# G formed in two runs of 1280 and 1024 columns from one W tile, where there were three pairs of 384

## The chip, the core and the metric

The kernel runs on one core of a Trainium2 chip. The core has five engines with queues of their own: TensorE (PE, matrix products into PSUM; PEld are its weight loads), VectorE (DVE), ScalarE (ACT), GpSimd (POOL, which also issues transfers) and SyncE (SP, which issues transfers and transposing transfers). They wait for each other through semaphores. The metric is the device time of one execution in microseconds (us), median over several runs; lower is better.

## What is computed

Two stages in one kernel. The first is attention between a sequence `x` (8 batches, 8 heads, 512 rows of 64) and a small state (32 rows per head); the second is a feed-forward layer with a maximum over three products, over 8 x 544 = 4352 rows:

```
scores  = x @ state.T / 8;   a  = softmax(scores);    xread = a  @ state
scores2 = state @ x.T / 8;   a2 = softmax(scores2);   sread = a2 @ x
rows    = concat(xread, sread), the heads side by side: 512 columns
h       = max(rows @ w1, rows @ w2, rows @ w3)        # 768 columns
out     = h @ w_out                                   # 512 columns
```

## The kernel before

The work goes batch by batch. The x rows take a short cut: `rows @ w_i` is `a @ (state @ w_i)`. So for each batch the kernel first forms **G**, the product of the state with w1, w2 and w3, and then multiplies the attention weights `a` with G.

*G.* The 768 columns of h are taken in six groups m of 128, and the three matrices i side by side, so G of a batch is 128 rows (4 heads x 32 state rows) by 2 halves g by 2304 columns. `g_cols(b, ms)` (L240) forms the columns of the groups in `ms`, 384 per group. Per group it takes a PSUM buffer of the tag "two" (two buffers, each of two banks), runs 8 matmuls of 64 rows by 32 columns (4 pairs of heads s, 2 halves g) that sit on different parts of the array (`tile_position`), and has ACT copy 128x768 to G in bf16. `defer` lets such a copy wait: it goes into `copies_due` and is run behind the next t0 copy in `maxout` (L291), or by `flush_copies` at the next `g_cols`. `g_cols_fast` (L263), used twice for batch 0, takes two buffers of the tag "pw" (four buffers of one bank) and has ACT copy one half and DVE the other.

*W.* The weights lie in four tiles `w_sb`, for the groups (0), (1), (2,3) and (4,5); in each, matrix i is a block of 128 or 256 columns. `w_cols(m)` gives the tile and the slice, and `load_w` (L90) loads them by POOL's queue, one transfer per matrix and tile.

*Products.* `x_maxout(b, m)` (L296) makes three products of 512 columns from G and the transposed weights aT into three "pw" buffers (`pw0`, `pw1`, `pw2`), each of two matmuls. ACT copies the first (t0, L290), DVE takes the maximum with the second (t1, L293) and with the third (ht, L294). `s_maxout(m)` does the same for the state rows of all batches at the end. `ffn_out(b, j)` (L306) multiplies ht with w_out in six matmuls into a "pw" buffer; ACT copies it to `osb` (L326), and POOL sends two such pieces off at a time.

*Attention.* `scores` (L165) multiplies x, transposed, with `bd`, the state laid out in blocks, into a "two" buffer, and ACT takes the exponential e. `softmax` sums on DVE (den, rden) and multiplies on POOL (a). `a_transpose_dma` turns a by a transposing transfer on SP. `sread` (L213) makes the state's read into a "pw" buffer, and DVE divides it (L227, L229). For batches 4 to 7 `states` (L129) turns the state by a transposing transfer, and POOL copies it into `bd` (L140).

*Order.* The order of all instructions is written out by hand. Batches 0 and 1 are started together, with transfers still coming in (L344 to L423). Then a loop over b = 2 to 7 (L426) has six slots: `x_maxout(b, m)` and, behind it, the pieces of slot m. With n = b + 1: slot 0 has `scores(n)`; slot 1 `softmax(n)`, `g_cols(b, (2, 3))` and `ffn_out(b-1, 0)`; slot 2 the transposing transfers, `g_cols(b, (4, 5))` and `ffn_out(b-1, 1)`; slot 4 `ffn_out(b-1, 2)`, `sread(n)` and `g_cols(n, (0, 1))`; slot 5 `ffn_out(b-1, 3)`. So G of a batch is formed in three pairs, the first of them ahead of the batch. For batch 2 the first pair stands in the written order (L411). In the last turn there is no next batch, and `s_maxout(m)` fills each slot.

Each engine runs its instructions in this order. A buffer of a tag is given again to a later tile once its last reader is done, so the tags "two" and "pw" make PE wait for copies.

Of the kernel before, what the change touches and what calls it, by code (L numbers as in the profile page):

```python
# [8 lines left out]
F32 = mybir.dt.float32  # L9
BF16 = mybir.dt.bfloat16  # L10
# [5 lines left out]
def kernel(  # L16
# [14 lines left out]
    nc = tc.nc  # L31

    B, H, S, D = x.shape
    _, _, Ns, _ = state.shape
# [8 lines left out]
    HS = H // 2  # L43
    NM = d_ff // 128
# [5 lines left out]
    wpool = ctx.enter_context(tc.tile_pool(name="weights", bufs=1))  # L50
    work = ctx.enter_context(tc.tile_pool(name="work", bufs=2))
    pp = ctx.enter_context(tc.tile_pool(name="pp", bufs=2, space=bass.MemoryType.PSUM))
    ctx.enter_context(tc.manual_schedule())
    dve, act, pool = nc.vector.tensor_copy, nc.scalar.copy, nc.gpsimd.tensor_copy
# [29 lines left out]
    nc.gpsimd.dma_start(out=x0_sb[1], in_=x0_heads(1))  # L84

    chunks = ((0, 1), (1, 2), (2, 4), (4, 6))
    w_sb = [wpool.tile([128, HS, 3, (m1 - m0) * 128], BF16, name=f"w{m0}") for m0, m1 in chunks]
    wout_sb = wpool.tile([128, NM, d_model], BF16, name="wout")

    def load_w(c, parts=(0, 1, 2)):  # L90
        m0, m1 = chunks[c]
        for i in parts:
            w = (moe_w1, moe_w2, moe_w3)[i]
            nc.gpsimd.dma_start(  # L94
                out=w_sb[c][:, :, i, :],
                in_=w.rearrange("(kk p) f -> p kk f", p=128)[:, :, m0 * 128:m1 * 128])

    def w_cols(m):
        c = [m0 <= m < m1 for m0, m1 in chunks].index(True)
        f = (m - chunks[c][0]) * 128  # L100
        return w_sb[c], slice(f, f + 128)

    load_w(0)
    load_w(1)
# [8 lines left out]
    ats = data.tile([128, B, HS, Ns], BF16, name="ats")  # L113
# [7 lines left out]
    def bd(b, h):  # L121
        return bds[b // 2][:, b % 2, h]
# [21 lines left out]
    xT, e, a, aT, G, ht, osb = {}, {}, {}, {}, {}, {}, {}  # L144

    def new(d, b, shape, name, bufs=2):
        d[b] = work.tile(shape, BF16, tag=name, bufs=bufs, name=name)
# [13 lines left out]
    def x_transpose_dma(b):  # L161
        new(xT, b, [128, H, 2, 128], "xT", bufs=3)
        nc.sync.dma_start_transpose(out=xT[b].rearrange("p h j t -> p (h j) t"), in_=x_sb[b][:, 0:XW])
# [42 lines left out]
    def a_transpose_dma(b):  # L206
        new(aT, b, [128, J, 2, 128], "aT", bufs=3)
        nc.sync.dma_start_transpose(
            out=aT[b].rearrange("p j g t -> p (j g) t"), in_=a[b].rearrange("p j g s n -> p (j g s n)"))
# [3 lines left out]
    def sread(b):  # L213

        p = pp.tile([128, 2, 2, D], F32, tag="pw", bufs=4, name="psr")
        for j in range(J):
            for g in range(2):
                for s in range(HS):
                    xj = xv[b][:, 2 * s + g, j, :]
                    both = bass.AP(xj.tensor, xj.offset,  # L220
                                   (xj.ap[0], (XW - ((2 * s + g) * J + j) * D, 2), (1, D)))
                    nc.tensor.matmul(  # L222
                        p[32 * s:32 * s + 32, g], e[b][:, j, g, s, :], both,
                        start=(j == 0 and g == 0), stop=(j == J - 1), skip_group_check=True,
                        tile_position=(0, 32 * s))
        rd = work.tile([128, 2, 1], F32, tag="rd", name="rd")
        nc.vector.reciprocal(out=rd, in_=p[:, :, 1, 0:1])  # L227
        sr = work.tile([128, 2, D], BF16, tag="sr", bufs=B, name="sr")
        nc.vector.tensor_mul(out=sr, in0=p[:, :, 0, :], in1=rd.to_broadcast((128, 2, D)))  # L229
        late.append(lambda: nc.sync.dma_start_transpose(  # L230
            out=ats[:, b].rearrange("p s n -> p (s n)"), in_=sr.rearrange("p g d -> p (g d)")))


    copies_due = []

    def flush_copies():
        while copies_due:
            copies_due.pop(0)()

    def g_cols(b, ms, copies=(nc.scalar.copy, nc.scalar.copy), defer=(False, False)):  # L240

        flush_copies()
        for m, copy, wait in zip(ms, copies, defer):
            if m == 0:
                new(G, b, [128, 2, NM * 384], "G", bufs=3)
            w, f = w_cols(m)
            p = pp.tile([128, 2, 512], F32, tag="two", name="pg")
            for s in range(HS):
                for g in range(2):
                    nc.tensor.matmul(  # L250
                        p[32 * s:32 * s + 32, g, 0:384].rearrange("p (i f) -> p i f", i=3),
                        bd(b, 2 * s + g)[64 * g:64 * g + 64, g, :], w[64 * g:64 * g + 64, s, :, f],
                        start=True, stop=True, tile_position=(64 * g, 32 * s))

            def place(m=m, p=p, copy=copy):
                copy(out=G[b][:, :, m * 384:(m + 1) * 384], in_=p[:, :, 0:384])  # L256

            if wait:
                copies_due.append(place)
            else:  # L260
                place()

    def g_cols_fast(b, m):  # L263

        if m == 0:
            new(G, b, [128, 2, NM * 384], "G", bufs=3)
        w, f = w_cols(m)
        p = [pp.tile([128, 512], F32, tag="pw", bufs=4, name=f"pgf{g}") for g in range(2)]
        for s in range(HS):
            for g in range(2):  # L270
                nc.tensor.matmul(
                    p[g][32 * s:32 * s + 32, 0:384].rearrange("p (i f) -> p i f", i=3),
                    bd(b, 2 * s + g)[64 * g:64 * g + 64, g, :], w[64 * g:64 * g + 64, s, :, f],
                    start=True, stop=True, tile_position=(64 * g, 32 * s))
        for g, copy in ((0, act), (1, dve)):
            copy(out=G[b][:, g, m * 384:(m + 1) * 384], in_=p[g][:, 0:384])  # L276


    def maxout(b, m, n, lhs, rhs, nk):
        if m == 0:  # L280
            new(ht, b, [128, NM, n], "ht", bufs=4)
        pw = []
        for i in range(3):
            p = pp.tile([128, 512], F32, tag="pw", bufs=4, name=f"pw{i}")
            for k in range(nk):
                nc.tensor.matmul(p[:, 0:n], lhs(i, k), rhs(k), start=(k == 0), stop=(k == nk - 1))  # L286
            pw.append(p)
        t0 = work.tile([128, 512], BF16, tag="t0", name="t0")
        t1 = work.tile([128, 512], BF16, tag="t1", name="t1")
        nc.scalar.copy(out=t0[:, 0:n], in_=pw[0][:, 0:n])  # L290
        if copies_due:  # L291
            copies_due.pop(0)()
        nc.vector.tensor_max(t1[:, 0:n], t0[:, 0:n], pw[1][:, 0:n])  # L293
        nc.vector.tensor_max(ht[b][:, m, :], t1[:, 0:n], pw[2][:, 0:n])  # L294

    def x_maxout(b, m):  # L296
        maxout(b, m, 512,
               lambda i, k: G[b][:, k, m * 384 + i * 128:m * 384 + i * 128 + 128],
               lambda k: aT[b][:, :, k, :], 2)

    def s_maxout(m):
        w, f = w_cols(m)
        maxout("s", m, B * Ns, lambda i, k: w[:, k, i, f], lambda k: ats[:, :, k, :], HS)


    def ffn_out(b, j, split=False):  # L306
# [73 lines left out]
    for b in range(2, B):  # L380
        nc.gpsimd.memset(x_sb[b][:, XW:XW + D], 1.0)
    sread(0)
    g_cols_fast(0, 2)
    g_cols(0, (3,))
    g_cols(1, (0,))
    x_maxout(0, 2)
    a_transpose(1, 0, act)
# [20 lines left out]
    x_transpose_dma(3)  # L408
    ffn_out(0, 0)
    x_maxout(1, 4)  # L410
    g_cols(2, (0, 1))  # L411
    ffn_out(0, 1)
    load_x(5)
    for k in range(2, B // 2):
# [11 lines left out]
    for b in range(2, B):  # L426
        n = b + 1
        slots = [[] for _ in range(NM)]
        if n < B:
            slots[0].append(lambda: scores(n, 0, 2))  # L430
            slots[1].append(lambda: softmax(n, 0, 2, nc.gpsimd.tensor_mul))
            slots[2].append(lambda: a_transpose_dma(n))
            if n % 2 and n + 1 < B:
                slots[2].append(lambda: states((n + 1) // 2, pool))
            if n + 2 < B:
                slots[2].append(lambda: x_transpose_dma(n + 2))
            slots[5].append(late_transposes)
            if n + 3 < B:
                slots[0].append(lambda: load_x(n + 3))
        else:  # L440
            for m in range(NM):
                slots[m].append(lambda m=m: s_maxout(m))
        slots[1].append(lambda: g_cols(b, (2, 3)))
        slots[2].append(lambda: g_cols(b, (4, 5)))
        if n < B:
            slots[4].append(lambda: sread(n))
            slots[4].append(lambda: g_cols(n, (0, 1), defer=(False, True)))
        for j, m in enumerate((1, 2, 4, 5)):
            slots[m].insert(0 if m > 2 else len(slots[m]), lambda j=j: ffn_out(b - 1, j))
        for m in range(NM):  # L450
            x_maxout(b, m)
            for f in slots[m]:
                f()
# [36 lines left out]
```

## Time and profile before

| | us |
|---|---|
| median of 11 runs | 160.05 (158.82 to 162.53) |
| the profiled execution | 159.75 |
| its span, first to last instruction | 157.9 |
| PE busy | 147.5 |
| ACT busy | 97.9 |
| DVE busy | 94.0 |
| POOL busy | 50.6 |
| ACT's copies of G, L256, 46 of 128x768 | 35.6, 805 ns each |
| PE's matmuls for G, L250, 368 of 384 columns | 12.1 |

The span is what the engines' records cover; the execution's time is 1.9 us longer. A row of the timeline has the start, the duration, the engine, the line, the operation with output and inputs, how many instructions it stands for and, in brackets, how long the engine was idle before it and whom it waited for. Rows of PE overlap by the depth of its pipeline: the distance between the starts of two rows, not the duration, is what the first cost. Records of some matmuls are missing, so "x5" can be six. A tile name without a number stands for all tiles of that name: pw for pw0 to pw2, t for t0 and t1.

### The profile page before, as it was taken

Reading aid. Unit: us, or ns where it says so; the run is one execution under the profiler, and the core shown is the slowest. Engines: PE = TensorE matmul, PEld = TensorE weight load, DVE = VectorE, ACT = ScalarE, POOL = GpSimd, SP = SyncE. Lnnn points to the kernel's source line nnn. Section 1 sums busy time; section 2 is a strip of 40 time slices with the busy share of each in tenths; the row PEclk is TensorE's granted clock in tenths of the full one; section 3 lists DMA queues with packets and bytes.
Section 4 is the critical chain, followed back from the end, with each engine's and each line's share of the span. In section 5 each row is a group of like instructions: output and inputs, shape, how many; then the busy total and the mean of one; then the engine's idle time right before and its main releaser. Section 6 shows DMA issues by size and latency. Waiting matters only on the chain.

```text
span 157.9 us, 3562 instructions
## 1 busy us (share of the span) xinstructions
PE 147.5 (93%) x1416; PEld 71.9 (46%) x1437; DVE 94.0 (60%) x161; ACT 97.9 (62%) x158; POOL 50.6 (32%) x72
## 2 busy tenths in 40 slices
PE   6887779999999999999999999999999999999990
PEld 2444433454544444434444444444434565566450
DVE  4775866768527674767476747574757484465200
ACT  3345677798837837783788378836874637733340
POOL 8998196000833405541004061501050100100150
PEclk9999999999999999999999999999999999999999
DMA  4999999999089999798730876070307030030365
GB/s 116 201 179 197 197 215 187 225 164 144 12 176 149 122 244 215 228 170 214 136 133 0 103 142 266 4 201 8 137 0 199 8 139 0 1 136 0 133 220 179
DMA packets 36720, 21.72 MB, mean 138 GB/s; under 512 B 21952, under 2 KB 34368, under 8 KB 36704
## 3 DMA queue, kind: packets, MB, share of 16 engines
q0 software_dynamic: 17216, 15.08, 49.5%
q1 hardware_dynamic: 19344, 6.29, 21.6%
q8 instruction: 11, 0.18, 0.5%
q10 hardware_dynamic: 144, 0.13, 0.2%
q14 instruction: 5, 0.04, 0.1%
HBM read 15.20 MB, written 8.91 MB: 153 GB/s over the span
## 4 chain that ended last, share of the span: by engine, by line
PE 81%; DMA 5%; DVE 4%; POOL 4%; ACT 2%; issue 2%; DVEq 0%; POOLq 0%
PE pw L286 42%; PE po L323 27%; PE pg L250 6%; DMA x<-in_x_dram 5%; POOL w L94 3%; PE psr L222 3%; PE ps L177 2%; DVE t L293 2%; ACT t L290 1%; DVE ht L294 1%; PE ph L315 1%; DVE den L189 1%; ACT xT L159 1%; POOL x L84 1%; PE pxt L156 0%
## 5 line engine op out<-in xcount | busy, mean ns | idle before, releaser
L286 PE MATMUL pw<-aT,G 128*128 128x512 bf16 x288 | 69.5, 380 | 1.6 <-DVE G L276 0.9
L293 DVE TENSOR_TENSOR t<-t,pw 128x512 bf16<-128x512 bf16 (+1 forms) x54 | 35.1, 650 | 39.7 <-ACT t L290 34.4
L323 PE MATMUL po<-wout,ht 128*128 128x512 bf16 x178 | 45.6, 380 | 0.8
L286 PEld LDWEIGHTS <-G 128*128 128x128 bf16 x288 | 26.9, 98 | 34.6 <-issue 3.7
L256 ACT CAST G<-pg 128x768 bf16<-128x768 f32 x46 | 35.6, 805 | 9.0 <-PE pg L250 8.6
L294 DVE TENSOR_TENSOR ht<-t,pw 128x512 bf16<-128x512 bf16 (+1 forms) x54 | 35.5, 658 | 6.0 <-DVE t L293 0.5
L290 ACT CAST t<-pw 128x512 bf16<-128x512 f32 (+1 forms) x54 | 30.6, 566 | 9.1 <-PE pw L286 8.3
L326 ACT COPY osb<-po 128x512 f32<-128x512 f32 x33 | 19.3, 585 | 22.9 <-PE po L323 14.6
L323 PEld LDWEIGHTS <-ht 128*128 128x128 bf16 x198 | 18.2, 98 | 23.8 <-issue 4.0
L192 POOL TENSOR_TENSOR a<-e,rden 128x1024 bf16<-128x1024 bf16 (+1 forms) x9 | 14.5, 1618 | 39.6 <-DVE rden L191 29.3
L335 POOL DMA_DIRECT2D out_dram<-osb x14 | 8.0, 569 | 45.3 <-ACT osb L326 36.3
L250 PE MATMUL pg<-w,bd 64*32 64x384 bf16 x368 | 12.1, 328 | 0.1
L189 DVE TENSOR_REDUCE den<-e 128x32 f32<-128x1024 bf16 (+1 forms) x10 | 9.9, 991 | 0.8 <-ACT e L182 0.8
L94 POOL DMA_DIRECT2D w<-in_moe_w_dram x12 | 9.2, 787 | 0.0
L286 PE MATMUL pw<-ats,w 128*128 128x256 bf16 x72 | 8.8, 273 | 0.0
L182 ACT ACTIVATE e<-ps 128x1024 bf16<-128x1024 f32 x6 | 6.1, 1023 | 3.8 <-PE ps L177 3.8
L140 POOL COPY bd<-stT 64x512 bf16<-64x512 bf16 x4 | 4.3, 1066 | 11.8 <-DMA stT<-st 11.7
L286 PEld LDWEIGHTS <-w 128*128 128x128 bf16 x72 | 7.1, 98 | 2.1
L118 PE MATMUL idle<-zero 128*128 128x512 bf16 x18 | 6.5, 503 | 1.2 <-DVE zero L81 1.2
L250 PEld LDWEIGHTS <-bd 64*32 64x32 bf16 x368 | 3.4, 89 | 7.0 <-issue 5.8
L70 POOL DMA_DIRECT2D x<-in_x_dram x7 | 6.3, 911 | 0.7 <-DMA x<-in_x_dram 0.7
L222 PE MATMUL psr<-x,e 128*32 128x128 bf16 x256 | 5.0, 220 | 1.0
(49 smaller groups left out, 67.9 us busy)
## 6 DMA issues: line engine op xcount, KB each, us to landing
out_dram<-osb POOLq DMA_DIRECT2D x14, 512.0 KB, 3.6
x<-in_x_dram POOLq DMA_DIRECT2D x7, 512.0 KB, 11.0
w<-in_moe_w_dram POOLq DMA_DIRECT2D x6, 256.0 KB, 8.8
w<-in_moe_w_dram POOLq DMA_DIRECT2D x6, 128.0 KB, 5.9
wout<-in_moe_w_out_dram POOLq DMA_DIRECT2D x1, 768.0 KB, 10.3
x0f<-in_x_dram SPq DMA_DIRECT2D x1, 512.0 KB, 4.0
out_dram<-osb SPq DMA_DIRECT2D x1, 512.0 KB, 2.7
stf<-in_state_dram POOLq DMA_DIRECT2D x3, 128.0 KB, 9.4
```

Of the source, the lines that this page charges most:

```text
L94: nc.gpsimd.dma_start(out=w_sb[c][:, :, i, :], in_=w.rearrange("(kk p) f -> p kk f", p=128)[:, :, m0 * 128:m1 * 128])
L189: nc.vector.reduce_sum(out=den, in_=e[b][:, :, g0:g1], axis=AX.X)
L192: mul(out=a[b][:, :, g0:g1].rearrange("p j g s n -> p j (g s) n"), in0=e[b][:, :, g0:g1].rearrange("p j g s n -> p j (g s) n"), in1=rden.r ...
L222: nc.tensor.matmul(p[32 * s:32 * s + 32, g], e[b][:, j, g, s, :], both, start=(j == 0 and g == 0), stop=(j == J - 1), skip_group_check=Tru ...
L250: nc.tensor.matmul(p[32 * s:32 * s + 32, g, 0:384].rearrange("p (i f) -> p i f", i=3), bd(b, 2 * s + g)[64 * g:64 * g + 64, g, :], w[64 * ...
L256: copy(out=G[b][:, :, m * 384:(m + 1) * 384], in_=p[:, :, 0:384])
L286: nc.tensor.matmul(p[:, 0:n], lhs(i, k), rhs(k), start=(k == 0), stop=(k == nk - 1))
L290: nc.scalar.copy(out=t0[:, 0:n], in_=pw[0][:, 0:n])
L293: nc.vector.tensor_max(t1[:, 0:n], t0[:, 0:n], pw[1][:, 0:n])
L294: nc.vector.tensor_max(ht[b][:, m, :], t1[:, 0:n], pw[2][:, 0:n])
L323: nc.tensor.matmul(p, ht[b][:, m, j * 128:(j + 1) * 128], wout_sb[:, m, :], start=(m == 0), stop=(m == NM - 1))
L326: act(out=o[:, j, :], in_=p)
```

## The change

W becomes one tile of 2304 columns per row, in which the four chunks follow each other; within a chunk the three matrices stand in blocks as before. G takes the same layout: in the chunks (2,3) and (4,5) a group's 384 columns are three blocks of 128, 256 apart. `m_cols(t, m)` gives them for W and for G.

With columns in one order for W and G, a piece of G can be any stretch of columns. `g_piece(b, c0, c1, copy, wait)` forms one: up to 512 columns in a "two" buffer, with one copy of both halves, or up to 256 in two "pw" buffers, with two copies.

For batches 2 to 7, `g_front(b)` forms columns 0 to 1280 in pieces of 512, 512 and 256 (copied by ACT, by ACT deferred, and by DVE), where `g_cols(b, (0, 1))` stood; `g_back(b)` forms 1280 to 2304 in two pieces of 512 (ACT, and ACT deferred) in slot 1. Slot 2 forms no G any more. A batch has 40 matmuls for G and not 48.

Batches 0 and 1 keep their pairs, and their copies now write three blocks of 128 per half for groups 2 to 5. For batch 0, group 2 is formed by `g_cols` and no longer by `g_cols_fast`, so ACT copies both halves of it.

```diff
-    w_sb = [wpool.tile([128, HS, 3, (m1 - m0) * 128], BF16, name=f"w{m0}") for m0, m1 in chunks]
+    w_sb = wpool.tile([128, HS, NM * 384], BF16, name="w")
+    def w_slices(t, c):
+        m0, m1 = chunks[c]
+        return t[:, :, 384 * m0:384 * m1].rearrange("p a (i mf) -> p a i mf", i=3)
+    def m_cols(t, m):
+        c = [m0 <= m < m1 for m0, m1 in chunks].index(True)
+        f = (m - chunks[c][0]) * 128
+        return w_slices(t, c)[:, :, :, f:f + 128]
...
+    def g_piece(b, c0, c1, copy, wait=False):
+        if c0 == 0:
+            new(G, b, [128, 2, NM * 384], "G", bufs=3)
+        n = c1 - c0
+        if n > 256:
+            p = pp.tile([128, 2, 512], F32, tag="two", name="pg")
+            ps = [p[:, g, 0:n] for g in range(2)]
+        else:
+            ps = [pp.tile([128, n], F32, tag="pw", bufs=4, name=f"pgs{g}") for g in range(2)]
+        for s in range(HS):
+            for g in range(2):
+                nc.tensor.matmul(
+                    ps[g][32 * s:32 * s + 32],
+                    bd(b, 2 * s + g)[64 * g:64 * g + 64, g, :], w_sb[64 * g:64 * g + 64, s, c0:c1],
+                    start=True, stop=True, tile_position=(64 * g, 32 * s))
+        def place():
+            if n > 256:
+                copy(out=G[b][:, :, c0:c1], in_=p[:, :, 0:n])
+            else:
+                for g in range(2):
+                    copy(out=G[b][:, g, c0:c1], in_=ps[g])
...
-                copy(out=G[b][:, :, m * 384:(m + 1) * 384], in_=p[:, :, 0:384])
+                copy(out=m_cols(G[b], m), in_=pv)
...
+    def g_front(b):
+        flush_copies()
+        g_piece(b, 0, 512, act)
+        g_piece(b, 512, 1024, act, True)
+        g_piece(b, 1024, 1280, dve)
+    def g_back(b):
+        flush_copies()
+        g_piece(b, 1280, 1792, act)
+        g_piece(b, 1792, 2304, act, True)
...
-               lambda i, k: G[b][:, k, m * 384 + i * 128:m * 384 + i * 128 + 128],
+               lambda i, k: m_cols(G[b], m)[:, k, i],
...
-    g_cols_fast(0, 2)
-    g_cols(0, (3,))
+    g_cols(0, (2, 3))
     g_cols(1, (0,))
...
-    g_cols(2, (0, 1))
+    g_front(2)
...
-        slots[1].append(lambda: g_cols(b, (2, 3)))
-        slots[2].append(lambda: g_cols(b, (4, 5)))
+        slots[1].append(lambda: g_back(b))
...
-            slots[4].append(lambda: g_cols(n, (0, 1), defer=(False, True)))
+            slots[4].append(lambda: g_front(n))
```

More of the change, by code (lines that the diff above doesn't have):

```diff
@@ L92, in load_w @@
         for i in parts:
[L93 to L101, printed above, removed]
+            w = (moe_w1, moe_w2, moe_w3)[i].rearrange("(kk p) f -> p kk f", p=128)
+            nc.gpsimd.dma_start(out=w_slices(w_sb, c)[:, :, i, :], in_=w[:, :, m0 * 128:m1 * 128])
     load_w(0)
@@ L238, in flush_copies, with g_cols @@
             copies_due.pop(0)()
-    def g_cols(b, ms, copies=(nc.scalar.copy, nc.scalar.copy), defer=(False, False)):
+    def g_piece(b, c0, c1, copy, wait=False):
[19 more added lines that the diff above has]
+                    copy(out=G[b][:, g, c0:c1], in_=ps[g])
+        if wait:
+            copies_due.append(place)
+        else:
+            place()
+    def g_cols(b, ms, copies=(act, act), defer=(False, False)):
         flush_copies()
@@ L245, in g_cols @@
                 new(G, b, [128, 2, NM * 384], "G", bufs=3)
-            w, f = w_cols(m)
             p = pp.tile([128, 2, 512], F32, tag="two", name="pg")
+            pv = p[:, :, 0:384].rearrange("p g (i f) -> p g i f", i=3)
             for s in range(HS):
@@ L250, in g_cols, with place @@
                     nc.tensor.matmul(
-                        p[32 * s:32 * s + 32, g, 0:384].rearrange("p (i f) -> p i f", i=3),
-                        bd(b, 2 * s + g)[64 * g:64 * g + 64, g, :], w[64 * g:64 * g + 64, s, :, f],
+                        pv[32 * s:32 * s + 32, g], bd(b, 2 * s + g)[64 * g:64 * g + 64, g, :],
+                        m_cols(w_sb, m)[64 * g:64 * g + 64, s],
                         start=True, stop=True, tile_position=(64 * g, 32 * s))
-            def place(m=m, p=p, copy=copy):
-                copy(out=G[b][:, :, m * 384:(m + 1) * 384], in_=p[:, :, 0:384])
+            def place(m=m, pv=pv, copy=copy):
+                copy(out=m_cols(G[b], m), in_=pv)
             if wait:
@@ L266, in g_cols_fast @@
             new(G, b, [128, 2, NM * 384], "G", bufs=3)
-        w, f = w_cols(m)
         p = [pp.tile([128, 512], F32, tag="pw", bufs=4, name=f"pgf{g}") for g in range(2)]
@@ L272, in g_cols_fast @@
                     p[g][32 * s:32 * s + 32, 0:384].rearrange("p (i f) -> p i f", i=3),
-                    bd(b, 2 * s + g)[64 * g:64 * g + 64, g, :], w[64 * g:64 * g + 64, s, :, f],
+                    bd(b, 2 * s + g)[64 * g:64 * g + 64, g, :], m_cols(w_sb, m)[64 * g:64 * g + 64, s],
                     start=True, stop=True, tile_position=(64 * g, 32 * s))
         for g, copy in ((0, act), (1, dve)):
-            copy(out=G[b][:, g, m * 384:(m + 1) * 384], in_=p[g][:, 0:384])
+            copy(out=m_cols(G[b], m)[:, g], in_=p[g][:, 0:384].rearrange("p (i f) -> p i f", i=3))
     def maxout(b, m, n, lhs, rhs, nk):
@@ L297, in x_maxout @@
         maxout(b, m, 512,
-               lambda i, k: G[b][:, k, m * 384 + i * 128:m * 384 + i * 128 + 128],
+               lambda i, k: m_cols(G[b], m)[:, k, i],
                lambda k: aT[b][:, :, k, :], 2)
     def s_maxout(m):
-        w, f = w_cols(m)
-        maxout("s", m, B * Ns, lambda i, k: w[:, k, i, f], lambda k: ats[:, :, k, :], HS)
+        maxout("s", m, B * Ns,
+               lambda i, k: m_cols(w_sb, m)[:, k, i],
+               lambda k: ats[:, :, k, :], HS)
     def ffn_out(b, j, split=False):
```

## The prediction

> **What bounds the kernel.** I read the busy table of the page first, then busy time by stage, then the timeline of one batch, then the start.
>
> ```profile
> PE 147.5 (93%) x1416; PEld 71.9 (46%) x1437; DVE 94.0 (60%) x161; ACT 97.9 (62%) x158; POOL 50.6 (32%) x72
> ```
>
> TensorE (PE) is busy for 93%. The stages say where the other 7% lie (columns: window, its length, busy time of PE, weight loads, DVE, ACT, POOL, clock, DMA):
>
> ```profile
> 18.00:26.03 8.03, 6.19 (x74) 2.54 (x61) 5.26 (x12) 5.67 (x10) 6.69 (x14) 1.00 1.39 202
> 46.28:61.92 15.64, 15.39 (x155) 6.95 (x156) 9.79 (x16) 10.88 (x17) 4.27 (x4) 1.00 1.29 189
> 93.23:108.88 15.65, 15.40 (x155) 6.97 (x157) 9.98 (x17) 10.88 (x17) 4.37 (x5) 1.00 0.44 132
> ```
>
> A batch of the loop takes 15.65 us, and PE works in 15.40 of them at full clock; DVE and ACT have 5 us to spare. So in the loop a change is worth what it takes from PE's own sequence. Before 26 us PE waits for others. The timeline shows what PE's sequence loses:
>
> ```profile
> 95.00 1.46 PE L286 MATMUL pw<-aT,G 128*128 128x512 bf16 x6
> 96.38 0.52 PE L250 MATMUL pg<-w,bd 64*32 64x384 bf16 x16
> 96.84 1.47 PE L323 MATMUL po<-wout,ht 128*128 128x512 bf16 x5
> ...
> 101.29 2.75 PE L286 MATMUL pw<-aT,G 128*128 128x512 bf16 x12
> 103.88 1.24 PE L323 MATMUL po<-wout,ht 128*128 128x512 bf16 x5
> ...
> 105.83 0.52 PE L250 MATMUL pg<-w,bd 64*32 64x384 bf16 x16
> 106.28 1.47 PE L286 MATMUL pw<-aT,G 128*128 128x512 bf16 x6
> ```
>
> Twelve matmuls of 512 columns take 103.88-101.29 = 2.59 us, 0.216 each. Six from 95.00 therefore stream until 96.30. The pair of G pieces starts at 96.38, 0.09 later, and the next matmul starts 0.46 after that: a pair costs 0.55 us. Its eight matmuls per piece run side by side, so its columns need only 2 x 384 x 0.216/512 = 0.32. The other **0.22-0.23 us go at the borders of the run**.
>
> **The change, part by part.**
>
> *Two runs for three pairs (batches 2 to 7).* Is the border paid per run or per piece? A run of one piece is in the trace: G of (1,1) starts at 22.59, the next matmul at 22.88. That is 0.29 for 0.16 of columns, 0.13 over, just what the pair has behind it (0.46-0.32). So it is per run. Per batch: before 3 x 0.55 = 1.65; after, the same 2304 columns (0.97) plus two borders (2 x 0.23) = 1.43. I take 0.22 saved in each of 6 batches, **-1.3 us**. If borders went by pieces (5 for 6), it would be 0.11 each, -0.66: the weak end.
>
> *ACT.* Six copies of 128x768 at 805 ns become four of 128x1024. That cast is not in the trace; 128x512 costs 590 and 128x768 805, so I take 1.02 us, which the exponential of 128x1024 (1023 ns) confirms. ACT falls by 0.7 us a batch and was not the bound: worth nothing by itself. The front's first copy now delays t0 of x_maxout(b,5) by 0.2-0.3 us; its PSUM buffer is wanted again only by x_maxout(b+1,0), 1.3 us after it is free, and G's own copies are finished over 1 us before they are read. In the back run only the third product of x_maxout(b,2) reads the new copy.
>
> *DVE.* Two casts of 128x256 a batch are added. Nearest rows: the 128x256 copy at L318, 425 ns; 128x384 at L276, 553. I take 0.42, between 0.42 and 0.55. They take two of the four "pw" buffers. On the clock of batch 5: run from 105.83, pieces 0.22 apart, the small one from 106.28, the next full matmul at 106.50 (106.28 before). The copies can start some 0.36 after the small piece (ACT's first copy starts 0.43 after its 384-column piece), at 106.64, and end at 107.06 and 107.48. The third product of x_maxout(5,5), at 106.50+4x0.216 = 107.36, waits for the first, ffn_out(4,3), at 107.80, for the second: covered by 0.3 us each. Without that cover each late 0.1 us costs 0.6 over six fronts.
>
> [...]
>
> *The first front (batch 2)* stands where DVE is behind:
>
> ```profile
> 39.31 0.52 PE L250 MATMUL pg<-w,bd 64*32 64x384 bf16 x16
> 39.47 0.63 DVE L293 TENSOR_TENSOR t<-t,pw 128x512 bf16<-128x512 bf16 x1
> ```
>
> With two buffers taken, ffn_out(0,1) gets the one that this t1 reads. It ends at 40.10, while the longer run would let PE go on at 39.98 (39.76 before): 0.15 lost. Then the deferred copy (1.02) stands ahead of the aT copy on ACT, which ffn_out(0,2) needs for its buffer: about 0.1 more. **+0.25 us**; ends 0 and 0.4.
>
> *G(0,2) without the fast form.*
>
> ```profile
> 18.73 0.36 PE L271 MATMUL pgf<-w,bd 64*32 64x384 bf16 x8 [0.54 <-DMA w<-in_moe_w_dram]
> 19.15 0.48 ACT L276 CAST G<-pgf 128x384 bf16<-128x384 f32 x1 [0.80 <-PE pgf L271]
> 20.36 0.55 DVE L276 CAST G<-pgf 128x384 bf16<-128x384 f32 x1
> 20.96 1.25 PE L286 MATMUL pw<-aT,G 128*128 128x512 bf16 x5 [0.89 <-DVE G L276]
> 21.39 0.58 ACT L290 CAST t<-pw 128x512 bf16<-128x512 f32 x1 [0.36 <-PE pw L286]
> 22.48 1.07 ACT L204 COPY aT<-pat 128x512 bf16<-128x512 bf16 x2 [0.50 <-PE pat L203]
> ```
>
> PE waits here for the half that DVE copies late. After the change ACT copies it all from 19.15 to 19.95. G(1,0) now waits for that, since "two" has two buffers, and x_maxout(0,2) starts at 19.95+0.05+0.29 = 20.3 and not 20.96. ACT is late next: three copies 0.69 apart put t0 at 21.22, not 21.39. The second half of a_transpose(1) waits for its end, 21.8, and starts at 21.87, not 22.22; behind it ACT's chain (aT, aT, G(1,1), t0) runs without a gap, from 22.0 and not 22.48. PE's matmuls up to 26.04 hang on that chain: **-0.48 us**. These copies of batches 0 and 1 write runs of 128 columns, a form that no row shows: the strided copy xT<-pxt (128x1024) takes 1012 ns beside 1023 for a contiguous 1024, so I add nothing; at most 0.22 each (as if of 1024), three in this chain, which would turn the term into +0.2.
>
> *W in one tile.* In the built program's order no engine waits for another DMA than before, POOL and SP have the same sequence, and each transfer has the same rows and sizes: 0. Strides of W and G alone change.
>
> *What is late next.* PE now runs ahead of what hangs on fixed latencies:
>
> ```profile
> 61.01 2.19 POOL L140 COPY bd<-stT 64x512 bf16<-64x512 bf16 x2 [6.12 <-DMA stT<-st]
> 63.25 0.63 PE L177 MATMUL ps<-bd,xT 128*128 128x64 bf16 x16
> ```
>
> scores(4) starts at 63.25, 0.05 after POOL finishes bd of batches 4 and 5 at 63.20: this wait has no slack now. bd hangs by fixed steps (POOL's a at 52.98, two transposing DMAs, 6 us) on rden(3) at 52.5, which is ahead of the runs saved in batch 2. So batch 2's share waits here and is lost: **+0.25 us**, or 0 if the DMAs come sooner. The second such place (POOL from 91.82 to 94.0, scores(6) at 94.53) has 0.5 us of slack and keeps 0.3.
>
> **Sum:** -1.3 + 0.25 - 0.48 + 0.25 = -1.3 us. The profiled execution took 159.75 us, 157.9 of it span: 158.45. Its time lies 0.3 under the median of 160.05; from the median it is 158.75. I say **158.6**.
>
> **Rivals.**
>
> *Hidden (within 0.5%).* PE arrives earlier only to wait: both bd places and the early chain (+0.2 for -0.48) eat the gain, or borders go by pieces: -0.66 + 0.25 + 0.2 + 0.25 = 0.0: 159.8 by the profiled execution, 160.1 by the median. For it: scores(4) has no slack, and before 26 us ACT and DMA lead. Against it: from batch 3 on nothing but PE is short. Chance 0.26.
>
> *Slower.* The small pieces hold two of the four "pw" buffers, and DVE's two copies become what ffn_out(b,3) waits for. The cover is 0.3 us for both copies; the gain is gone when that matmul is 0.22 late, copies of 0.68 us each. At 0.82 each it is 0.5 late in six fronts: +3.0-1.3, 161.4. For it: a 128x512 operation on DVE takes 0.69. Against it: 0.42 in the nearest row. Chance 0.11.
>
> *More than forecast.* If bd comes sooner and DVE is on time at 39.5, the two losses of batch 2 are not there: -1.3-0.48 = -1.8, 158.0. Chance 0.08. That the change doesn't do what it says, pieces that are not in a row, is excluded: the built program has 24 and 16 matmuls with nothing between.
>
> The forecast holds 0.55. Faster by over 0.5% (0.8 us, about what a measurement of this kernel can tell from no change) is 0.55+0.08 = 0.63, the same 0.26, slower 0.11. The range must take in -1.8 from the lower half of the runs shown (159.1) and the hidden case: 157.3 to 160.0. It leaves out the slower case and little else.
>
> **What would show it.** Right: the loop's batches from 4 on take 15.43 us; PE is 0.67 (front) and 0.56 (back) from a run's start to the next matmul; x_maxout(0,2) begins near 20.3 and the run of G(0,4) and G(0,5) near 25.55 (26.04 before); PE waits for POOL's bd at about 63. Wrong: a gap ahead of x_maxout(b,5)'s third product or of ffn_out(b,3), a batch of 15.65, casts of 128x256 over 0.6 us, or strided casts well over 805 ns.

## The result and the profile after

| | before | after |
|---|---|---|
| median of 47 and 12 runs, us | 160.19 | 158.52 |
| ratio of the two, 95% interval | | 0.9897 [0.9864, 0.9930] |
| the profiled execution | 159.75 | 158.48 |
| its span | 157.9 | 156.7 |

The medians are of all runs, and the ratio leaves out those in a slower state, of which the changed kernel had three of 12: 160.04, 160.95 and one of 254.13 us, at a granted clock of 0.56.

The forecast was 158.6 us, with 1.3 us saved. 158.52 lies within its range, and the ratio puts the saving at 1.03%, some 1.65 us, with an interval of 1.1 to 2.2 us, clear of zero. But a sum can come out right with wrong terms, so each is looked up in the trace. First the busy table on the page of the changed kernel:

```profile
PE 146.8 (94%) x1373; PEld 72.6 (46%) x1389; DVE 97.9 (62%) x172; ACT 94.1 (60%) x146; POOL 50.5 (32%) x72
```

PE has 48 matmuls less (six batches with 40 for 48) and is busy 0.7 us less. DVE has 3.9 us more (before 94.0), ACT 3.8 less (before 97.9). That ACT and DVE changed places was worth nothing by itself; the stages show what was. Busy time by stage, in the changed kernel, with the columns as before (window, length, PE, weight loads, DVE, ACT, POOL, clock, DMA); the windows are the same stretches of work:

```profile
18.40:25.98 7.58, 6.09 (x71) 2.72 (x59) 4.77 (x11) 5.86 (x10) 6.28 (x14) 1.00 1.35 190
46.70:62.11 15.41, 15.31 (x147) 7.01 (x148) 10.49 (x18) 10.24 (x15) 5.62 (x6) 1.00 1.26 196
92.92:108.33 15.41, 15.31 (x147) 7.00 (x148) 10.72 (x19) 10.24 (x15) 3.00 (x3) 1.00 0.46 142
```

A batch takes 15.41 us where it took 15.65. The timeline of batch 5, the same stretch as the one shown of before:

```profile
96.08 0.62 PE L255 MATMUL pg<-w,bd 64*32 64x512 bf16 x16
96.64 1.47 PE L365 MATMUL po<-wout,ht 128*128 128x512 bf16 x5
...
105.07 0.62 PE L255 MATMUL pg<-w,bd 64*32 64x512 bf16 x16
105.51 0.29 PE L255 MATMUL pgs<-w,bd 64*32 64x256 bf16 x8
105.74 1.47 PE L327 MATMUL pw<-aT,G 128*128 128x512 bf16 x6
107.04 1.46 PE L365 MATMUL po<-wout,ht 128*128 128x512 bf16 x5
```

The back run costs 96.64-96.08 = 0.56 to the next matmul, the front run 105.74-105.07 = 0.67. Six products from 105.74 take 1.30 = 6 x 0.216, so nothing waits in front of the third product, and 107.04 follows at once, so ffn_out(b,3) doesn't wait either.

The timeline of the start in the changed kernel:

```profile
19.13 0.52 PE L281 MATMUL pg<-w,bd 64*32 64x384 bf16 x16 [0.56 <-DMA w<-in_moe_w_dram]
20.40 0.36 PE L281 MATMUL pg<-w,bd 64*32 64x384 bf16 x8 [0.75 <-ACT G L287]
20.69 1.47 PE L327 MATMUL pw<-aT,G 128*128 128x512 bf16 x6
25.98 0.52 PE L281 MATMUL pg<-w,bd 64*32 64x384 bf16 x16
```

W arrives at 19.13, 0.40 later than in the execution shown of before (18.73). The wait for DVE's half of G is gone, and G(0,4) and G(0,5) start 25.98-19.13 = 6.85 after W's arrival, before 26.04-18.73 = 7.31. (W's arrival stands here for the start of the first matmul of G(0,2).)

The first front in the changed kernel's timeline:

```profile
39.26 0.63 PE L255 MATMUL pg<-w,bd 64*32 64x512 bf16 x16
39.41 0.63 DVE L334 TENSOR_TENSOR t<-t,pw 128x512 bf16<-128x512 bf16 x1
40.09 1.46 PE L365 MATMUL po<-wout,ht 128*128 128x512 bf16 x6
...
42.55 1.03 ACT L262 CAST G<-pg 128x1024 bf16<-128x1024 f32 x1
43.45 0.62 ACT L207 COPY aT<-pat 128x512 bf16<-128x512 bf16 x1
44.12 2.75 PE L365 MATMUL po<-wout,ht 128*128 128x512 bf16 x11
```

From the front's start to the next matmul it is 0.83 and not 0.67: ffn_out(0,1) waits 0.16 for the buffer that this t1 reads. The deferred copy at 42.55 stands ahead of the aT copy. From the front to scores(3) it is 8.74, before 8.26.

And the place where bd was to be late, in the changed kernel's timeline:

```profile
59.78 2.19 POOL L143 COPY bd<-stT 64x512 bf16<-64x512 bf16 x2 [4.47 <-DMA stT<-st]
63.41 0.63 PE L180 MATMUL ps<-bd,xT 128*128 128x64 bf16 x16
```

POOL is done 1.4 us ahead of scores(4). This wait isn't there in this execution.

### The profile page after: what moved, and what is told of

Its sections match the earlier page's. It is cut to its first block, busy times and chain, and to the rows that moved or that the text cites. A ratio compares the mean times of both kernels' runs of the same rounds, so it can differ in the third digit from the quotient of the medians.

```text
span 156.7 us, 3468 instructions
## 1 busy us (share of the span) xinstructions
PE 146.8 (94%) x1373; PEld 72.6 (46%) x1389; DVE 97.9 (62%) x172; ACT 94.1 (60%) x146; POOL 50.5 (32%) x72
## 4 chain that ended last, share of the span: by engine, by line
PE 80%; ACT 6%; DMA 5%; DVE 4%; issue 2%; POOL 1%; DVEq 0%; ACTq 0%; POOLq 0%
PE pw L327 39%; PE po L365 27%; DMA w<-in_moe_w_dram 5%; PE pg L255 4%; PE idle L121 3%; PE psr L225 2%; ACT t L331 2%; ACT G L287 2%; DVE t L334 2%; PE ps L180 1%; DVE den L192 1%; PE pg L281 1%; ACT e L185 1%; PE ph L357 1%; POOL a L195 1%
## 5 line engine op out<-in xcount | busy, mean ns | idle before, releaser
L365 PE MATMUL po<-wout,ht 128*128 128x512 bf16 x183 | 46.6, 380 | 0.9
L368 ACT COPY osb<-po 128x512 f32<-128x512 f32 x33 | 19.3, 585 | 29.8 <-PE po L365 29.8
L365 PEld LDWEIGHTS <-ht 128*128 128x128 bf16 x198 | 18.8, 98 | 23.9 <-issue 2.8
L262 ACT CAST G<-pg 128x1024 bf16<-128x1024 f32 x24 | 24.5, 1022 | 3.8 <-PE pg L255 3.2
L287 ACT CAST G<-pg 128x768 bf16<-128x768 f32 x11 | 8.7, 808 | 3.0 <-PE pg L281 2.9
L255 PE MATMUL pg<-w,bd 64*32 64x512 bf16 x192 | 7.5, 381 | 0.0
L180 PEld LDWEIGHTS <-xT 128*128 128x128 bf16 x128 | 4.8, 98 | 2.5 <-DVE xT L162 0.8
```

The source lines that it names most:

```text
L255: nc.tensor.matmul(ps[g][32 * s:32 * s + 32], bd(b, 2 * s + g)[64 * g:64 * g + 64, g, :], w_sb[64 * g:64 * g + 64, s, c0:c1], start=True, ...
L262: copy(out=G[b][:, :, c0:c1], in_=p[:, :, 0:n])
L287: copy(out=m_cols(G[b], m), in_=pv)
L365: nc.tensor.matmul(p, ht[b][:, m, j * 128:(j + 1) * 128], wout_sb[:, m, :], start=(m == 0), stop=(m == NM - 1))
L368: act(out=o[:, j, :], in_=p)
```

## The experiments

Each kernel was timed beside runs of the kernel before on its own chip; the ratio is to those, and medians are of the runs shown. Kernels are compared with each other by these ratios.

| kernel | median us | before us | ratio, 95% interval |
|---|---|---|---|
| e1_layout | 160.48 | 160.56 | 0.9998 [0.9953, 1.0043] |
| e2_no_fast | 159.56 | 160.56 | 0.9969 [0.9931, 1.0007] |
| e3_runs_only | 159.05 | 160.56 | 0.9925 [0.9882, 0.9968] |
| e4_halves | 158.38 | 160.56 | 0.9891 [0.9836, 0.9945] |
| e5_front_later | 157.95 | 159.93 | 0.9890 [0.9831, 0.9949] |
| e6_copies_twice | 160.05 | 159.93 | 1.0009 [0.9961, 1.0057] |
| e9_three_runs | 162.47 | 160.83 | 1.0152 [1.0093, 1.0210] |
| e10_states_early | 165.68 | 160.83 | 1.0262 [1.0169, 1.0355] |
| e11_after_again | 158.81 | 160.83 | 0.9897 [0.9836, 0.9958] |
| e12_states_apart | 158.89 | 160.75 | 0.9875 [0.9805, 0.9945] |

**The theory:** the border of a run is paid per run, so two runs for three save 0.22 us a batch; the form of G(0,2) brings some 0.5 at the start; two waits in batch 2 take 0.5 back. **The rivals:** borders go by pieces or matmuls; the layout of W does something; the small pieces' buffers cost what the border saves.

### One part alone: layout, G(0,2), runs

e1_layout keeps the three pairs and the fast form, on W in one tile. e2_no_fast adds G(0,2) without the fast form. e3_runs_only has the two runs, but the fast form kept.

```diff
# e1_layout, against after
-    g_cols(0, (2, 3))
+    g_cols_fast(0, 2)
+    g_cols(0, (3,))
-    g_front(2)
+    g_cols(2, (0, 1))
-        slots[1].append(lambda: g_back(b))
+        slots[1].append(lambda: g_cols(b, (2, 3)))
+        slots[2].append(lambda: g_cols(b, (4, 5)))
-            slots[4].append(lambda: g_front(n))
+            slots[4].append(lambda: g_cols(n, (0, 1), defer=(False, True)))
# e2_no_fast: the same without the first hunk; e3_runs_only: the first hunk alone
```

> The layout alone: W in one tile, G in its order, the pairs of 384 and the fast form of G(0,2) as before. My theory: nothing on PE moves and the strided casts of 128x768 take what contiguous ones took (805 ns), so the same time as before, 0 +- 0.3 us. Rival (one W tile ties matmuls to later transfers, or strided casts are slower): over 0.5 us slower, with a wait of PE for a W transfer or casts over 850 ns.

> The layout and G(0,2) formed by the ordinary form, but the pairs of 384 in batches 2 to 7. My theory: counted from the arrival of W for G(0,2), the run of G(0,4) starts 0.45 us earlier than before (6.85 us after it and not 7.30), and as the bd wait at scores(4) has no slack, 0.2 to 0.45 us of it reach the end. Rival (that stretch is set by the transfers, not by the copies): no gain, 0.

> The two runs in batches 2 to 7, but G(0,2) in the fast form as before. My theory: six batches by 0.22 us less 0.25 us in the first front gives 1.05 us faster, 0.8 if the bd wait takes the share of batch 2. Rival (the gain came from G(0,2)): less than 0.5 us faster.

The layout alone changes nothing that can be told (0.9998), and all 46 casts of its profile take 799 to 817 ns, 805 in the mean, though those of four groups in six write in blocks. G(0,2) alone gives 0.31%, 0.5 us, though its interval reaches over 1; the runs alone 0.75%, 1.2 us. Together 1.06%, and the change gives 1.03%: **the two parts add up.** In the profiles, the batches of e2_no_fast take 15.64 and those of e3_runs_only 15.41, so the whole gain per batch belongs to the runs. In e2_no_fast G(0,4) starts 6.85 after W's arrival, in e3_runs_only 7.91.

That last number tells how the old form works. In before, its repetition (e7_before_again) and e3_runs_only, W came 1.90, 1.38 and 1.14 after the start of scores(1), but G(0,4) started 9.21, 9.05 and 9.05 after it: with the fast form the start hangs on DVE's work for batch 1, behind which its half of G is copied, and a W that comes earlier against scores(1) helps little. Behind W that makes 7.31, 7.67 and 7.91. In the new form it is 6.85 or 6.86 behind W in all ten profiles, with W from 17.76 to 19.32. So the term of -0.48 is -0.46 in the first case, and -0.82 and -1.06 in the others. (The fourth profile with the fast form, that of e1_layout, ran part of this stretch at a lower clock; see the last section.)

e2_no_fast also shows the wait that the profile of the changed kernel didn't, in its timeline:

```profile
63.62 0.63 PE L180 MATMUL ps<-bd,xT 128*128 128x64 bf16 x16 [0.55 <-POOL bd L143]
```

### What is a border paid for: rounds, pieces, runs

e4_halves makes each piece of 512 in two rounds of 256 columns, so a batch has 72 matmuls for G and not 40, in the same runs and buffers.

```diff
-        for s in range(HS):
-            for g in range(2):
-                nc.tensor.matmul(
-                    ps[g][32 * s:32 * s + 32],
-                    bd(b, 2 * s + g)[64 * g:64 * g + 64, g, :], w_sb[64 * g:64 * g + 64, s, c0:c1],
+        for k in range(0, n, 256):
+            for s in range(HS):
+                for g in range(2):
+                    nc.tensor.matmul(
+                        ps[g][32 * s:32 * s + 32, k:k + 256],
+                        bd(b, 2 * s + g)[64 * g:64 * g + 64, g, :],
+                        w_sb[64 * g:64 * g + 64, s, c0 + k:c0 + k + 256],
```

> The changed kernel with each piece of 512 columns made of two rounds of matmuls of 256: the same runs, columns and copies, 72 matmuls per batch for 40. My theory (borders are paid per run): 0.01 us for each of the 4 added rounds in six batches, 0.2 to 0.3 us slower than the changed kernel, 1.0 to 1.5 us faster than before. Rival (borders are paid per round of matmuls): 0.11 us x 4 x 6 = 2.6 us slower than the changed kernel, slower than before.

Batch 5 in its timeline:

```profile
95.69 0.63 PE L256 MATMUL pg<-w,bd 64*32 64x256 bf16 x32
96.25 1.47 PE L367 MATMUL po<-wout,ht 128*128 128x512 bf16 x6
...
104.69 0.63 PE L256 MATMUL pg<-w,bd 64*32 64x256 bf16 x32
...
105.36 1.47 PE L329 MATMUL pw<-aT,G 128*128 128x512 bf16 x6
```

The runs take 0.56 and 0.67, as in the changed kernel, with nearly twice the matmuls, and the ratio shows none of the 0.2 to 0.3 us expected for the added rounds (0.9891 and 0.9897). A round of eight has no price of its own; the rival that counts matmuls is out.

e9_three_runs cuts the back run in two, one piece each. Pieces and matmuls per batch stay at 5 and 40; there are three runs again.

```diff
-        slots[1].append(lambda: g_back(b))
+        slots[1].append(lambda: (flush_copies(), g_piece(b, 1280, 1792, act)))
+        slots[2].append(lambda: (flush_copies(), g_piece(b, 1792, 2304, act, True)))
```

> The changed kernel with its back run cut in two: columns 1280 to 1792 in slot 1, 1792 to 2304 in slot 2, each a run of one piece. Pieces (5), matmuls (40), copies and casts per batch stay. Theory (the border is paid per run): one border more per batch, 0.22 us, so a batch takes 15.62 to 15.65 us in place of 15.41, each one-piece run costs 0.22 + 0.22 = 0.44 us to the next matmul, and the whole 6 x 0.22 = 1.3 us more than the changed kernel: ratio to the kernel before 0.996 to 0.998, like the one with pairs and without the fast form. Rival (the gain lies in fewer pieces and matmuls, 5 and 40 for 6 and 48): batch 15.41 as in the changed kernel, ratio 0.988 to 0.991.

It is 3.7 us slower than the changed kernel beside it (162.47 against 158.81), three times what the border explains. A batch takes 16.17, 0.76 more. Batch 5 in its timeline:

```profile
95.93 1.46 PE L327 MATMUL pw<-aT,G 128*128 128x512 bf16 x6
97.32 0.41 PE L255 MATMUL pg<-w,bd 64*32 64x512 bf16 x8
97.66 1.47 PE L365 MATMUL po<-wout,ht 128*128 128x512 bf16 x6
...
100.35 0.41 PE L255 MATMUL pg<-w,bd 64*32 64x512 bf16 x8
100.70 1.47 PE L365 MATMUL po<-wout,ht 128*128 128x512 bf16 x6
102.00 1.89 PE L327 MATMUL pw<-aT,G 128*128 128x512 bf16 x8
104.25 1.04 PE L327 MATMUL pw<-aT,G 128*128 128x512 bf16 x4 [0.36 <-ACT G L262]
```

Both are in it. *The border:* six matmuls from 95.93 stream until 97.23, the run starts 0.09 later and the next matmul 0.34 behind its start: 0.43, and 0.44 at 100.35. Two such runs are 0.87 where the one of two pieces is 0.09+0.56 = 0.65. **0.22 for one border more, with pieces and matmuls the same:** the rival that counts pieces is out. *The rest:* eight matmuls from 102.00 end at 103.73, but the ninth starts at 104.25, 0.52 later. It is the second product of x_maxout(b,4), the first to read the piece from 1792 on, whose copy was deferred behind t0 of x_maxout(b,3). In the changed kernel that copy stands one slot earlier. 0.22+0.52 = 0.74 of the 0.76. My expectation had left out who reads the deferred piece. What the 0.22 us of a border consist of, no run here shows.

### The first front, moved

e5_front_later puts g_front(2) behind ffn_out(0,1), so that the front's buffers are free.

```diff
     x_maxout(1, 4)
-    g_front(2)
     ffn_out(0, 1)
+    g_front(2)
```

> The changed kernel with the first front (batch 2) behind ffn_out(0,1) and not ahead of it. My theory: the first front cost 0.25 us because ffn_out(0,1) waited for t1 of x_maxout(1,4); by then t1 and ht are done, so x_maxout(2,0) starts 0.1 to 0.25 us earlier against the start of x_maxout(1,4), and the total is up to 0.25 us lower than the changed kernel. Rival (the longer run itself costs it): no difference.

By the times it can't be told from the changed kernel. The milestones tell more: from x_maxout(1,4) to x_maxout(2,0) it is 45.52-36.70 = 8.82, in the changed kernel 46.70-37.87 = 8.83: nothing is won. Its timeline:

```profile
39.38 0.62 PE L255 MATMUL pg<-w,bd 64*32 64x512 bf16 x16
...
40.05 1.47 PE L327 MATMUL pw<-aT,G 128*128 128x512 bf16 x6
41.35 0.61 PE L206 MATMUL pat<-ident,a 128*128 128x128 bf16 x8
42.25 0.63 PE L225 MATMUL psr<-x,e 128*32 128x128 bf16 x32 [0.29 <-DVE t L334]
```

The front now takes 0.67 and the 0.16 is gone. But sread(2) starts 0.90 behind the transposes, in the changed kernel 0.75 (42.68 to 43.43): it waits for DVE's next t1, behind the two casts, at a buffer of the same tag. The loss moved 2 us down and stayed the same size, 0.15.

### The small pieces' copies, doubled

The rival for slower was that the two "pw" buffers are held too long. e6_copies_twice does each of DVE's casts twice.

```diff
-                for g in range(2):
+                for g in (0, 0, 1, 1):
                     copy(out=G[b][:, g, c0:c1], in_=ps[g])
```

> The changed kernel with each of DVE's copies of 128x256 done twice, 0.75 us more DVE time per front. The theory of the cover: the second copy ends at 0.35 to 0.4 us past the start of ffn_out(b,3), so PE waits about 0.4 us in each of six fronts, 2 to 2.5 us slower than the changed kernel, with the wait in front of ffn_out(b,3). Rival (DVE has 5 us to spare per batch, a copy more costs nothing): under 0.5 us.

1.0009 to before, so some 1.8 us slower than the changed kernel. PE and DVE in batch 5 of its timeline:

```profile
106.03 1.68 PE L327 MATMUL pw<-aT,G 128*128 128x512 bf16 x6
106.17 1.67 DVE L265 CAST G<-pgs 128x256 bf16<-128x256 f32 x4 [0.18 <-PE pgs L255]
107.55 1.46 PE L365 MATMUL po<-wout,ht 128*128 128x512 bf16 x6
```

The six products take 1.52 and not 1.30: the third, due at 106.03+4x0.216 = 106.89, waits for the first buffer, free at 106.17+2x0.42 = 107.0. That is 0.2 a batch, 15.61 for 15.41, 1.2 over six, and the other 0.6 of the difference is within what the ratios leave open; this profile also has a wait of 0.82 for bd. The place was not the one expected: ffn_out(b,3) follows at once, at 107.55, while the last cast ends at 107.84. So it doesn't use the second buffer; probably the buffers are handed out in another turn here, but the profile doesn't number them. The first buffer's cover is confirmed, though: 0.3 us were there, 0.42 more makes it late by 0.1 to 0.2. The rival is real, and was not in force.

### When bd comes

In three more profiles the wait at scores(4) came and went. e7_before_again and e8_after_again are the two kernels unchanged, one profile each; e11_after_again is the changed kernel once more.

> The kernel before once more, for its profile. My theory: the arrival of W for G(0,2) (18.73 us in the first profile) moves by some tenths from run to run with the start's transfers, and so does the landing of the state's transposing transfer ahead of scores(4); the distance from that arrival to the run of G(0,4) stays 7.3 us and a loop batch 15.65. Rival: the arrival is the same within 0.1 us, and the 0.4 us later arrival in the changed kernel's profile is the change's doing.

> The changed kernel once more, for its profile. My theory: arrival of W anywhere from 18.6 to 19.3, 6.85 us from it to the run of G(0,4), a loop batch 15.40, and PE waits at scores(4) for POOL's bd in some executions. Rival: arrival at 19.1 again.

> The changed kernel itself, beside the two others on the same chip. Both theories: ratio to the kernel before 0.986 to 0.993, batch 15.41 us; start of the run of G(0,4) and G(0,5) 6.85 us behind the arrival of W, whenever that is; bd of batches 4 and 5 done anywhere between 60 and 63.6 us.

e7_before_again took 159.03, its batches 15.64; its W came at 17.52, so the rival's fixed arrival fell, but so did the theory's fixed 7.3 to G(0,4), which was 7.67. e8_after_again took 158.94, its batches 15.41, with no wait. In e11_after_again (profiled 159.07) the wait is there, longer than ever:

```profile
63.73 0.63 PE L180 MATMUL ps<-bd,xT 128*128 128x64 bf16 x16 [1.20 <-POOL bd L143]
```

From scores(3) to scores(4) it is 17.09 and not 15.41: 1.68 lost, 0.33 of it at aT, whose transfer is late too (x_maxout(3,0) at 61.08), the rest at bd. W had come 1.37 earlier than in the profile of the changed kernel (17.76), so all that is won at the start is lost here, and 0.3 us more. The rows of DMA issues between 44 and 58 us (last number: us from issue to landing), first of the changed kernel's profile, then of its repetition:

```profile
x<-in_x_dram POOLq DMA_DIRECT2D x1, 512.0 KB, 9.8
...
stT<-st SPq DMA_TRANSPOSE x1, 3.1
```

```profile
x<-in_x_dram POOLq DMA_DIRECT2D x1, 512.0 KB, 13.3
...
stT<-st SPq DMA_TRANSPOSE x1, 6.2
```

Over eleven profiles, ordered by how long the load of x takes:

| load of x, us | 8.7 | 9.1 | 9.6 | 9.8 | 10.8 | 11.0 | 11.1 | 11.6 | 12.4 | 12.8 | 13.3 |
|---|---|---|---|---|---|---|---|---|---|---|---|
| stT, us | 2.5 | 2.5 | 2.7 | 3.1 | 4.0 | 4.2 | 4.2 | 4.7 | 5.4 | 5.7 | 6.2 |
| profile | e5 | e4 | e7 | after | e8 | e9 | e3 | before | e2 | e6 | e11 |
| PE waits for bd, us | 0 | 0 | 0 | 0 | 0 | 0 | 0 | 0 | 0.55 | 0.82 | 1.20 |

(The profile of e1_layout, with 11.0, 4.1 and no wait, fits in.) **The state's transfer lands late when the load of x does.** From 44 to 58 us in e11_after_again the packets of queue q0 take 65.4% and those of q1 60.7% of the 16 DMA engines' span (76.4% and 45.9% in the changed kernel's profile), together more than all of it. But neither this nor the table shows that the load is the cause: in the same profiles the transfer of aT, just ahead, goes from 3.2 to 7.0, and a 512 KB store of the output, issued just ahead of the load, from 7.5 to 11.4. The three are late together. Why the load takes 8.7 in one execution and 13.3 in another is not shown by any run.

Two kernels tried to take the state's transfers out of this place. Both issue them ahead of the loop; e10_states_early also moves POOL's copy to slot 0, e12_states_apart leaves it in slot 2.

```diff
+    def states_dma(k):
+        stT[k] = data.tile([128, 4, 128], BF16, name=f"stT{k}")
+        nc.sync.dma_start_transpose(out=stT[k], in_=st[k].rearrange("p t c d -> p (t c d)"))
...
     x_transpose_dma(4)
+    for k in range(2, B // 2):
+        states_dma(k)
...
# e10_states_early alone
-                slots[2].append(lambda: states((n + 1) // 2, pool))
+                slots[0].append(lambda: states((n + 1) // 2, pool))
```

> The changed kernel with the two transposing transfers of the state (batches 4 to 7) issued on SP ahead of the loop, and POOL's copies of them to bd in slot 0 in place of slot 2. Theory (the time from the transfer's issue to its landing varies, 2.5 to 5.8 us in the profiles so far, and the wait for bd at scores(4) is there only when it is long): PE never waits for bd; bd of batches 4 and 5 is done by about 50 us and not 60 to 63.5; the median lies 0 to 0.25 us under the changed kernel, too little to tell by the times, ratio 0.986 to 0.990. Rival (the wait is a fixed cost of the changed kernel, as predicted): 0.25 us under it in every execution, and the distance from the first G run of batch 2 to scores(4) and from scores(4) to scores(5) is 0.25 shorter.

It is 2.6% slower than the kernel before, 165.68, so the times of both expectations fell; only the wait for bd is gone, as the theory had it. POOL and PE in its timeline:

```profile
55.44 2.19 POOL L148 COPY bd<-stT 64x512 bf16<-64x512 bf16 x2 [7.63 <-DMA stT<-st]
...
58.53 1.91 POOL L200 TENSOR_TENSOR a<-e,rden 128x1024 bf16<-128x1024 bf16 x1
...
66.04 2.46 PE L332 MATMUL pw<-aT,G 128*128 128x512 bf16 x6 [4.31 <-DMA aT<-a]
```

bd is done at 57.63, earlier than in the changed kernel (61.97), but not by 50: SP issues the transfers at 51.00, behind that of xT. Meanwhile POOL waits 7.63 us for the transfer in its queue, and behind it stands softmax's a, which starts at 58.53 and not 53.41; aT follows, and PE waits 4.31 us for it. I had named PE's wait and not what stands behind POOL's.

> The changed kernel with the two transposing transfers of the state (batches 4 to 7) issued on SP ahead of the loop, where SP is idle, and POOL's copies to bd left in slot 2, so that POOL's order is that of the changed kernel. Theory (scores(4) waits in some executions because the state's transfer, issued in slot 2, lands late beside a load of x that takes 11 us or more): the transfer lands by about 55.5 us, POOL copies right behind its a, bd of batches 4 and 5 is done by about 57.5 us and never waited for; a run of the changed kernel loses 0 to 1.7 us there, so the median lies some 0.3 us under it, ratio 0.983 to 0.989. Rival (the earlier transfer only moves the delay to the transfer of aT or xT, which share the same engines, as in the kernel with POOL's copy in slot 0): PE waits for aT or xT at scores(4) or x_maxout(3,0), ratio over 0.990.

0.9875, where the changed kernel had 0.9897 in the runs before: no difference that can be told. The profiled execution, 161.53, is one of the two longest of six (157.46 to 161.71); it shows what can go wrong, and not what the other four lose here. POOL and PE in its timeline:

```profile
61.74 2.14 POOL L148 COPY bd<-stT 64x512 bf16<-64x512 bf16 x2 [7.41 <-DMA stT<-st]
...
63.37 2.71 PE L332 MATMUL pw<-aT,G 128*128 128x512 bf16 x6 [2.08 <-DMA aT<-a]
```

Issued at 51.36, the state's transfers land 9.9 us later, beside a load of x of 14.6, and the transfer of aT, behind them, takes 8.9. The expected landing at 55.5 fell; the rival's wait for aT is there, in this execution, but its ratio isn't. Whether an earlier or a later load of x would help wasn't tried. No version here beats the change by more than the runs can tell.

## Why the prediction was right, step by step

| term | forecast, us | in the runs |
|---|---|---|
| borders, six batches | -1.3 (0.22 each) | -1.4 (0.24 each) |
| first front, batch 2 | +0.25 | +0.26 |
| G(0,2) | -0.48 | -0.46 behind W, in a range to -1.06 |
| bd | +0.25 | 0 in this profile; 0 to 1.2 of wait in others |
| W in one tile | 0 | 0 (ratio 0.9998) |
| W's arrival | not a term | +0.40 between the two profiles |

*Borders.* Right, in size and in kind. 0.67 and 0.56 are the two numbers as forecast; 15.41 stands against 15.43. e9_three_runs gives the border by itself at 0.22, and e4_halves shows that the rounds cost nothing.

*ACT and DVE.* The groups of the changed kernel (busy, mean ns of one, idle before):

```profile
L262 ACT CAST G<-pg 128x1024 bf16<-128x1024 f32 x24 | 24.5, 1022 | 3.8 <-PE pg L255 3.2
L287 ACT CAST G<-pg 128x768 bf16<-128x768 f32 x11 | 8.7, 808 | 3.0 <-PE pg L281 2.9
L265 DVE CAST G<-pgs 128x256 bf16<-128x256 f32 x12 | 4.5, 419 | 0.9 <-PE pgs L255 0.9
```

1022 for the 1.02 read from the exponential, 419 for 0.42, and 808 for the copies of batches 0 and 1, eight of eleven strided, against 805: that they write blocks of 128 costs nothing. No run here has one cast of 512 columns on DVE in place of the two of 256.

*First front.* From the front to scores(3), 8.74-8.26 = 0.48, of which 0.22 is the third piece and 0.26 the loss, nearly all of it in two places: 0.16 at the buffer (0.83-0.67) and 0.12 from sread to ffn_out(0,2) (0.69 for 0.57), by the mechanisms that were named.

*G(0,2).* The mechanism was right (x_maxout(0,2) started 1.56 behind W, forecast 20.3-18.73 = 1.57), but G(0,4) came at 25.98 and not 25.55, because W came 0.40 later. The prediction took W's arrival as given; over the profiles it lies between 17.5 and 19.0 with the fast form, between 17.8 and 19.3 without. And it read the old form's time from one execution in which W came late against scores(1), the one that flatters the old form.

*bd.* The step that failed. "bd hangs by fixed steps", two transposing transfers and 6 us, was no fixed cost: the state's transfer takes 2.5 to 6.2 us. In the profile it cost 0, in e11_after_again 1.35, and 0.33 more at aT. The prediction's "0 if the DMAs come sooner" is what this profile shows; that they could also come later was not in it.

So the sum of -1.3 was met by the borders and the first front as computed (-1.43+0.26), an early gain that W's late arrival took back (-0.46+0.40), and a wait that wasn't there: -1.2, and 157.9 to 156.7 is the span's difference. A forecast loss of 0.25 that wasn't there and a W that came 0.40 late cancelled most of each other: that these two profiles differ by just the forecast 1.3 is luck in these two terms. The saving by the ratios, some 1.65 us, is that of e2_no_fast and e3_runs_only added up, so the saving itself isn't the luck of one execution; it is 0.35 more than the forecast, which the interval allows.

## What to carry to other kernels

Where PE is the bound, look at what it loses between rows: a run of small-tile matmuls cost 0.22 us at its borders with one, two or three pieces in it, so runs are to be counted, not matmuls or pieces. When a piece is moved or cut, look up who reads it first and what is queued behind its copy: two of the three experiments that lost time lost it there. The copies and casts came out as read from one execution's nearest rows (1022 ns for 1.02 us, 419 for 0.42), and the landing of a transfer did not (2.5 to 6.2 us); take a second profile before a transfer's landing becomes a fixed term.

## What was not expected of the hardware

*Transfers.* The same transposing transfer of the state took 2.5 to 6.2 us from issue to landing in kernels that issue it alike, in step with a 512 KB load on another queue, 8.7 to 13.3.

*The clock after a wait.* In e12_states_apart, busy time by window on both sides of the wait of 2.08 us (the last three columns: clock, DMA share, GB/s):

```profile
62.00:63.30 1.30, 0.00 (x0) 0.00 (x0) 0.00 (x0) 0.00 (x0) 1.24 (x2) 1.00 1.27 278
63.40:65.80 2.40, 2.40 (x6) 0.83 (x7) 0.46 (x1) 0.59 (x1) 2.40 (x4) 0.50 0.96 262
```

The six matmuls behind it run at half the clock and take 2.5 us for 1.3, so over a us goes there beyond the wait itself. Those behind the wait of 4.31 in e10_states_early take 2.25 us for 1.3, at a clock of 0.58 from 66 to 68. After the wait of 1.20 in e11_after_again the clock stayed at 1.00.

In another execution the clock was low behind a shorter wait. In the profile of e1_layout (161.41) PE waits 0.89 us for DVE's half of G(0,2), and what follows is slow; its row of the timeline, and the clock by slices of 4 us from its page:

```profile
21.21 2.31 PE L327 MATMUL pw<-aT,G 128*128 128x512 bf16 x5 [0.89 <-DVE G L317]
PEclk9999969999999999999999999999999999999999
```

The slice with the 6 lies from 19.95 to 23.94, and from the start of the five matmuls to the next row it is 23.32-21.21 = 2.11 us, in e3_runs_only 21.62-20.53 = 1.09. In the kernel before, the same five matmuls behind the same wait of 0.89 took 1.25 us at full clock (1.00 from 18.00 to 26.03), and in e3_runs_only and e7_before_again 1.25 us behind waits of 1.27 and 1.26. So the length of the wait alone doesn't decide, and no run here shows what does.
